# Second-layer expert weights laid out eight rows per partition, three experts moved as one transfer each

## The chip, the cores and the metric

The kernel runs on one core of a Trainium2 chip. The time is the device time of one execution in microseconds (us). In this document PE is TensorE, PEld its weight loads, DVE VectorE, ACT ScalarE, POOL GpSimd and SP SyncE, which issues every DMA (transfer) of this kernel. Less is better.

## The reference

An attention with 32 memory slots per head feeds a soft mixture of 8 experts. The change lies in the experts:

```python
    logits = x @ phi
    d = np.exp(logits - logits.max(0, keepdims=True))
    d /= d.sum(0, keepdims=True) + 1e-09
    slot_input = (d.T @ x).reshape(E, S_per_e, D)
    for e in range(E):
        h = np.maximum(slot_input[e] @ w1[e], 0.0)
        slot_out[e] = h @ w2[e]
    ...
    return (c @ slot_out).astype(np.float32)
```

Here x has 4608 rows of 512 columns, E is 8, each expert has 4 slots, w1[e] is 512 x 1024 and w2[e] is 1024 x 512, all float32. The two weight sets are 16 MB each. A slot row passes through w1, a ReLU and w2, and the output mixes the 32 slot rows for each of the 4608 rows.

## The kernel before

The kernel first runs attention and routing for four pairs of batches, then the experts, then the output. A planner (class Plan) takes all steps with estimated costs and a priority, simulates the engines, and emits each engine's instructions in the order it finds. A wait in front of an instruction holds everything behind it on its engine.

**First layer** (expert_in, L1383). Each expert's w1 comes as two transfers of 1 MB, 8 KB per partition. One transfer feeds 8 matmuls. The stationary operand is 32 columns wide, so a matmul uses one of four 32-column strips of the array, named by tile_position (0, 32 j); j picks which quarter of the 1024 hidden columns the strip makes. The moving operand of 256 columns is read from the weights in pairs of floats, one pair in every four floats.

**Second layer** (expert_out and mult, L1432). w2[e] comes in halves of 512 rows, four rows per partition, again 1 MB with 8 KB per partition. A half is multiplied twice, once for each half d of the 512 output columns: into kvbank for d = 0, into scbank for d = 1. I call one call of mult a product: four matmuls of 256 columns. In the kernel before its loop over k and j writes strip x = 2 k + j, so the four matmuls go to strips 0, 1, 2, 3. Each strip adds up its own partial sum over all experts, and slot_sums (L1347, L1355) adds the four strips up at the end.

**Tails.** The last NT = 5 of the 16 halves are loaded in pieces of 256 KB (tail_out): first ten pieces for d = 0, then ten for d = 1. The output for the first 256 columns can then start while the pieces for the others still arrive. The five d = 0 products close kvbank. Then PE does slot_sums(0), two direct outputs (L1572), and the outputs of six groups (out_mult, L1588) with the five d = 1 products placed between them by the table RIGHT. After the last of these slot_sums(1) follows, then the d = 1 outputs of the same groups, then 18 outputs of full width.

**Outputs.** ACT and DVE copy each output from its bank to a staging tile (L1564, L1565), and SP stores the tile (L1601). A group of three is stored as one transfer of 384 KB for each d. A store waits for its copies, and all stores and loads stand in one SP queue in the planner's order.

**Buffers.** The weight loads take slots of 2048 floats per partition (ws) in one arena; a slot is free again when the product that reads it has run. Loads rotate over eight semaphores, so a load also waits until the eighth load before it has landed.

Of the kernel before, what the change touches and what calls it, by code (L numbers as in the profile page):

```python
# [16 lines left out]
PE, DVE, ACT, POOL, SP = range(5)  # L17
# [253 lines left out]
def kernel(  # L271
# [27 lines left out]
    E, DM, FF = w1.shape  # L299
    NS = moe_phi.shape[1]  # L300
# [18 lines left out]
    add = plan.add  # L319
# [21 lines left out]
    W_SZ = 2048  # L341
# [12 lines left out]
    early = []  # L354
# [14 lines left out]
    def area(off, shape, n, below=(), fifo=False):  # L369

        size = shaped(off, shape)[1][1]
        xs = [shaped(off + i * size, shape) for i in range(n)]
        return Slots([a for a, _ in xs], [r for _, r in xs], below, fifo)
# [126 lines left out]
    def load(dst, src, nbytes, w, pri=None):  # L500
        add(
            SP, 0.06, lambda: nc.sync.dma_start(dst(), src), w=[w],  # L502
            dma=nbytes / {1 << 20: DMA_RATE, 1 << 18: HALF_RATE}.get(nbytes, IN_RATE), pri=pri, slack=SPREAD if nbytes == 1 << 18 else 0.0,
        )


# [781 lines left out]
    NW = (ARENA - small) // W_SZ  # L1288
    W0 = ARENA - NW * W_SZ
    ws = area(W0, [W_SZ], NW, early)  # L1290
    ots = area(W0, [OT_SZ], NOUT, [ws])
    b0 = W0 + NOUT * OT_SZ
    big = {6: area(b0, [6 * DM], 1, [ws]), 9: area(b0 + 6 * DM, [9 * DM], 1, [ws])}
    wqs = Slots(
        [qtile[:, i * W_SZ: i * W_SZ + W_SZ] for i in range(2)],
        [(TOP + i * W_SZ, W_SZ) for i in range(2)], [qs],
# [26 lines left out]

    EG = 4
    NT, NA = 5, 6
    RIGHT = (-1, 1, 1, 2, 2)
    SLOT_AT = (20.06, 20.08, 20.1)
    hTb = hTs.tile().split(E // EG)
# [3 lines left out]
    def load_w(src, pool=ws):  # L1332
        t = pool.tile()
        load(lambda: t.ap, src, 1 << 20, t)
        return t
# [38 lines left out]
    def expert_in(e, hb):  # L1374
        w1v = w1[e].rearrange("(i p z) f -> i p (z f)", i=2, z=2)
        w1b = [load_w(w1v[i], wqs if e == EG else ws) for i in range(2)]
        for i in range(2):

            def f(i=i):
                wv = w1b[i].ap.rearrange("p (c f) -> p c f", c=2)  # L1380
                for c in range(2):
                    for j in range(4):
                        nc.tensor.matmul(  # L1383
                            hb.ap[NS * j: NS * j + NS, :256],
                            SIM.ap[:, 2 * i + c, NS * e: NS * e + NS],
                            wv[:, c, 512 * (j // 2): 512 * (j // 2) + 512].rearrange(
                                "p (x u t) -> p x u t", u=2, t=2
                            )[:, :, j % 2, :],
                            start=(e % EG == 0 and i == 0 and c == 0),
                            stop=(e % EG == EG - 1 and i == 1 and c == 1),  # L1390
                            tile_position=(0, NS * j),
                        )

            add(PE, (0.9, 32), f, r=[SIM, w1b[i]], w=[hb])
# [27 lines left out]

    tails = []

    def mult(dst, e, i, t, d):
        u = 2 * e + i
        wide = t.ap.rearrange("p (j t d) -> p j t d", j=2, t=2)
        for k in range(2):
            for j in range(2):

                x = 2 * k + j
                nc.tensor.matmul(  # L1432
                    dst[NS * x: NS * x + NS, :HD],
                    hT()[:, 4 * k + 2 * i + j, NS * e: NS * e + NS],
                    wide[:, j, k, d * HD: d * HD + HD],
                    start=(u == 0),
                    stop=(u == 2 * E - 1),
                    tile_position=(0, NS * x),
                )

    def expert_out(e):
        w2v = w2[e].rearrange("(i p x) d -> p i (x d)", i=2, x=4)
        for i in range(2):
            t = ws.tile()
            if 2 * e + i >= 2 * E - NT:
                tails.append((e, i, t.split(4)))
                continue
            load(
                lambda t=t: t.ap, w2v[:, i], 1 << 20, t,
            )  # L1450
            for d in range(2):
                add(
                    PE, (0.45, 16),
                    lambda d=d, e=e, i=i, t=t: mult(pacc[d].ap[:, 0], e, i, t, d),
                    r=[hTb.part(e // EG), t], w=[pacc[d]],
                )

    def tail_out():
        for d in range(2):
            for e, i, t in tails:  # L1460
                w2h = w2[e].rearrange("(i p j t) d -> p i j t d", i=2, j=2, t=2)
                for j in range(2):
                    load(
                        lambda j=j, d=d, t=t: t.ap.rearrange("p (j t d) -> p j t d", j=2, t=2)[
                            :, j, :, d * HD: d * HD + HD
                        ],
                        w2h[:, i, j, :, d * HD: d * HD + HD], 1 << 18, t.part(2 * d + j),
                    )

    def tail_mult(d, n, after=()):  # L1470
        e, i, t = tails[n]
        return add(
            PE, (0.45, 16), lambda: mult(pacc[d].ap[:, 0], e, i, t, d),
            r=[hTb.part(e // EG), t.part(2 * d), t.part(2 * d + 1)], w=[pacc[d]], after=after,
        )


# [210 lines left out]
```

## Time and profile before

| what | value |
|---|---|
| time of the kernel, median of 3 runs | 201.5 us (201.01 to 202.52) |
| profiled execution, first to last instruction (its span) | 199.7 us |
| PE busy | 169.6 us, 85% of the span |
| DVE busy | 141.1 us, 71% |
| transfers moved | 76.47 MB, mean 383 GB/s |

The profile has no time of its own for the profiled execution beside its span; the median of the runs is 1.8 us longer than that span. The page cuts the span into 40 slices and gives for each the busy share of every engine and of the 16 DMA engines. "Chain" is the chain of waits that ended last, followed back from the last instruction. A float32 matmul stands in the trace as two records, one for each of two passes, each with a weight load of its own; the rows count records. The end of a matmul record is modelled, its start is not. In a view by windows the count of a window holds every instruction that was running in it.

### The profile page before, as it was taken

The page shows a single profiled execution, that of the slowest core. Times are in us where ns is not written, and L with a number is a line of the kernel's source. Part 1 is how long each engine was busy: PE and PEld are TensorE (multiplying, and loading weights), DVE is VectorE, ACT ScalarE, POOL GpSimd, SP SyncE. Part 2 cuts the span into 40 slices and gives each one's busy share as a digit, 9 for nine tenths or more (in the row PEclk, how much of TensorE's full clock was granted, in tenths as well). Part 3 has the DMA queues.
Part 4 walks back from the last instruction along what each step waited for, and adds up shares of the span by engine and source line. Part 5 has one row for each costly group of instructions (what it writes and reads, how often), then busy time and mean ns, then how long its engine had stood idle before and what let it go on. Part 6 is the DMA issues. An engine that isn't in the chain of part 4 may idle for free.

```text
span 199.7 us, 6103 instructions
## 1 busy us (share of the span) xinstructions
PE 169.6 (85%) x2607; PEld 109.4 (55%) x2607; DVE 141.1 (71%) x267; ACT 74.5 (37%) x191; POOL 95.6 (48%) x92
## 2 busy tenths in 40 slices
PE   7999737978879899787999799799999998999900
PEld 6777534544547487464666357565756633467500
DVE  7822631499999899899899997378999800658810
ACT  2032314436371755606553243110229500356600
POOL 7189303489995994889963276100016950000000
PEclk9999996699999999999999999999999999999965
DMA  6999999999999999999999999999999999999995
GB/s 200 366 391 395 382 384 390 381 390 381 402 364 388 391 379 403 382 390 404 420 422 410 415 420 420 417 423 427 415 418 425 365 322 328 344 317 344 398 447 255
DMA packets 32075, 76.47 MB, mean 383 GB/s; under 512 B 2097, under 2 KB 15921, under 8 KB 28337
## 3 DMA queue, kind: packets, MB, share of 16 engines
q1 hardware_dynamic: 32048, 76.09, 100.4%
q8 instruction: 20, 0.33, 0.7%
q14 instruction: 7, 0.05, 0.1%
HBM read 66.65 MB, written 9.44 MB: 381 GB/s over the span
## 4 chain that ended last, share of the span: by engine, by line
PE 34%; DMA 25%; POOL 16%; DVE 9%; issue 5%; SPq 4%; ACT 2%; POOLq 0%; DVEq 0%; ACTq 0%
DMA arena<-in_moe_w_dram 12%; DMA arena<-in_v_dram 9%; PE bank L1588 6%; POOL arena L871 5%; POOL arena L669 4%; POOL arena L848 4%; PE scbank L813 4%; DMA arena<-in_phi_dram 4%; PE bank L882 4%; PE kvbank L704 4%; SPq L502 4%; PE bank L1383 4%; POOL arena L648 3%; PE bank L1010 2%; PE scbank L1432 1%
## 5 line engine op out<-in xcount | busy, mean ns | idle before, releaser
L648 POOL TENSOR_TENSOR arena<-arena 128x1152 f32<-128x1152 f32 x8 | 21.0, 2631 | 17.1 <-ACT arena L641 14.0
L591 DVE STREAM_TRANSPOSE arena<-top 128x1152 f32<-128x1152 f32 x16 | 21.6, 1354 | 8.2 <-DMA top<-in_q_dram 8.2
L520 PE MATMUL kvbank<-ones 128*128 128x256 f32 x82 | 24.6, 439 | 2.4 <-ACT arena L728 1.3
L704 PE MATMUL kvbank<-arena 64*32 64x128 f32 x1152 | 20.7, 273 | 6.6 <-ACT arena L657 2.6
L669 POOL TENSOR_TENSOR arena<-arena 128x128 f32<-128x128 f32 (+2 forms) x32 | 23.4, 730 | 3.2 <-ACT arena L657 1.3
L813 PE MATMUL scbank<-arena 64*64 64x288 f32 x256 | 23.1, 434 | 2.1 <-DVE arena L827 2.0
L1526 POOL TENSOR_TENSOR cT<-cS,cT 32x640 fp32r<-32x640 f32 (+1 forms) x8 | 11.3, 1416 | 26.1 <-ACT cT L1521 25.7
L871 POOL TENSOR_TENSOR arena<-arena,ssm 128x576 f32<-128x576 f32 x16 | 18.3, 1151 | 9.6 <-DVE ssm L867 7.9
L848 POOL TENSOR_TENSOR arena<-arena,smx 128x576 f32<-128x576 f32 x16 | 18.4, 1151 | 8.0 <-DVE smx L843 8.0
L704 PEld LDWEIGHTS kvbank<-arena 64*32 64x32 f32 x1152 | 16.1, 105 | 10.9 <-issue 4.7
L606 DVE TENSOR_REDUCE arena<-arena 128x128 f32<-128x1152 f32 x8 | 17.1, 2146 | 4.6 <-DMA arena<-in_phi_dram 4.6
L520 PEld LDWEIGHTS kvbank<-ones 128*128 128x128 f32 x82 | 16.5, 216 | 6.4 <-ACT arena L728 1.7
L882 PE MATMUL bank<-arena 128*128 128x288 f32 x64 | 18.6, 423 | 1.0 <-DVE arena L874 0.8
L1565 DVE COPY arena<-bank 128x256 f32<-128x256 f32 (+1 forms) x30 | 14.4, 510 | 4.9 <-PE bank L1588 4.3
L827 DVE STREAM_TRANSPOSE arena<-scbank 128x576 f32<-128x576 f32 x16 | 12.2, 763 | 6.3 <-PE scbank L813 6.2
L1588 PE MATMUL bank<-sr,cT 64*128 64x256 f32 (+1 forms) x100 | 15.1, 358 | 0.4 <-ACT arena L1564 0.2
L813 PEld LDWEIGHTS scbank<-arena 64*64 64x64 f32 x256 | 9.6, 138 | 9.9 <-DVE arena L827 3.3
L853 ACT ACTIVATE arena<-arena 128x576 f32<-128x576 f32 x16 | 10.9, 684 | 10.3 <-POOL arena L848 10.3
L882 PEld LDWEIGHTS bank<-arena 128*128 128x128 f32 x64 | 11.2, 189 | 5.9 <-issue 1.7
L1588 PEld LDWEIGHTS bank<-sr,cT 64*128 64x128 f32 x100 | 9.9, 184 | 6.5 <-DVE arena L1565 4.1
L1564 ACT COPY arena<-bank 128x256 f32<-128x256 f32 (+1 forms) x24 | 10.4, 445 | 8.2 <-PE bank L1588 7.1
L1383 PE MATMUL bank<-arena,SIM 128*32 128x256 f32 x224 | 13.2, 390 | 0.2 <-DVE SIM L1264 0.2
(135 smaller groups left out, 266.4 us busy)
## 6 DMA issues: line engine op xcount, KB each, us to landing
arena<-in_moe_w_dram SPq DMA_DIRECT2D x25, 1024.0 KB, 13.7
top<-in_q_dram SPq DMA_DIRECT2D x8, 1152.0 KB, 11.4
arena<-in_k_dram SPq DMA_DIRECT2D x8, 1152.0 KB, 10.3
arena<-in_v_dram SPq DMA_DIRECT2D x8, 1152.0 KB, 12.7
arena<-in_moe_w_dram SPq DMA_DIRECT2D x20, 256.0 KB, 5.8
arena<-in_phi_dram SPq DMA_DIRECT2D x8, 576.0 KB, 6.8
out_dram<-arena SPq DMA_DIRECT2D x10, 384.0 KB, 4.4
out_dram<-arena SPq DMA_DIRECT2D x1, 2304.0 KB, 8.1
```

The costliest lines, as they stand in the source:

```text
L520: lambda: nc.tensor.matmul(warm.ap, ones, ones.unsqueeze(1).to_broadcast([P, 2, P]), start=True, stop=True,),
L591: lambda: nc.vector.transpose(qT.ap.rearrange("p (i u y) -> p u i y", i=2, y=Y), qt.ap[:, h * QT_SZ: h * QT_SZ + QT_SZ].rearrange("p (u i ...
L606: lambda: nc.vector.tensor_reduce(mx.ap[:, c0:c1], ph().rearrange("p c j m -> p c m j"), axis=AX.X, op=ALU.max),
L648: lambda: nc.gpsimd.tensor_tensor(ph(), ph(), mb.ap[:, c0:c1].unsqueeze(2).to_broadcast([P, c1 - c0, J, M]), op=ALU.subtract,),
L669: plus = lambda o, x, y: nc.gpsimd.tensor_tensor(o, x, y, op=ALU.add)
L704: nc.tensor.matmul(acc.ap[M * c: M * c + M, a, : 2 * D], ph()[h0: h0 + HALF, c, j, :], kv()[h0: h0 + HALF, :, c, j * D: j * D + D], start= ...
L813: nc.tensor.matmul(scb.ap[HALF * g: HALF * g + HALF, a, :JY], pair[g].kd.ap[h0: h0 + HALF, i, c].rearrange("p r m -> p (r m)"), pair[g].qT ...
L848: lambda: nc.gpsimd.tensor_tensor(exv(), exv(), bc(mx), op=ALU.subtract),
L871: lambda: nc.gpsimd.tensor_tensor(exv(), exv(), bc(sm), op=ALU.mult),
L882: nc.tensor.matmul(lp.ap[:, :JY], vpb.ap[:, h, :], aT.ap[:, a * JY: (a + 1) * JY], start=(h == 0), stop=(h == H - 1),)
L1383: nc.tensor.matmul(hb.ap[NS * j: NS * j + NS, :256], SIM.ap[:, 2 * i + c, NS * e: NS * e + NS], wv[:, c, 512 * (j // 2): 512 * (j // 2) + ...
L1588: nc.tensor.matmul(po.ap[:, : x.stop - x.start], cT[bp].ap[y: y + HALF, j // 2 * P: j // 2 * P + P], sr.ap[y: y + HALF, t, x], start=(t == 0),
```

## The change

w2[e] is now laid out with eight rows per partition: partition p holds rows 8 p to 8 p + 7, 16 KB without a break. Half h of an expert is then not 512 rows of the matrix but the first or the second four rows of every partition.

- Experts 0 and 1 (ONES = 2) still come as two transfers of 1 MB each, into two ws slots.
- Experts 2, 3 and 4 come as one transfer of 2 MB each, 16 KB per partition, into one slot of the new pool w2s, which lies over two neighbouring ws slots.
- Expert 5 takes a w2s slot too. Its first half comes as 1 MB; its second half and experts 6 and 7 come as the same twenty 256 KB pieces as before, now from rows that are 16 KB apart in memory instead of 8 KB.
- So that hidden unit and weight row meet, the first layer reads one pair in every eight floats (j = 4 groups of pairs), and mult takes its weights and strips in another way: product (e, h, d) writes strips x = 2 h and 2 h + 1, each for k = 0 and for k = 1.

The number of matmuls, weight loads, copies and bytes is the same. There are three transfers fewer.

```diff
@@ -1288,9 +1288,10 @@
     NW = (ARENA - small) // W_SZ
     W0 = ARENA - NW * W_SZ
     ws = area(W0, [W_SZ], NW, early)
-    ots = area(W0, [OT_SZ], NOUT, [ws])
+    w2s = area(W0, [2 * W_SZ], NW // 2, [ws, *early])
+    ots = area(W0, [OT_SZ], NOUT, [w2s])
     b0 = W0 + NOUT * OT_SZ
-    big = {6: area(b0, [6 * DM], 1, [ws]), 9: area(b0 + 6 * DM, [9 * DM], 1, [ws])}
...
+    ONES = 2
...
@@ -1383,9 +1385,7 @@
                         nc.tensor.matmul(
                             hb.ap[NS * j: NS * j + NS, :256],
                             SIM.ap[:, 2 * i + c, NS * e: NS * e + NS],
-                            wv[:, c, 512 * (j // 2): 512 * (j // 2) + 512].rearrange(
-                                "p (x u t) -> p x u t", u=2, t=2
-                            )[:, :, j % 2, :],
+                            wv[:, c].rearrange("p (x j t) -> p x j t", j=4, t=2)[:, :, j, :],
                             start=(e % EG == 0 and i == 0 and c == 0),
                             stop=(e % EG == EG - 1 and i == 1 and c == 1),
                             tile_position=(0, NS * j),
...
@@ -1422,56 +1422,70 @@
 
     tails = []
 
-    def mult(dst, e, i, t, d):
-        u = 2 * e + i
-        wide = t.ap.rearrange("p (j t d) -> p j t d", j=2, t=2)
+    def mult(dst, e, h, t, d):
+        n = 2 if e < ONES else 4
+        wide = t.ap.rearrange("p (j t d) -> p j t d", j=n, t=2)
         for k in range(2):
-            for j in range(2):
-
-                x = 2 * k + j
+            for x in range(2 * h, 2 * h + 2):
                 nc.tensor.matmul(
                     dst[NS * x: NS * x + NS, :HD],
-                    hT()[:, 4 * k + 2 * i + j, NS * e: NS * e + NS],
-                    wide[:, j, k, d * HD: d * HD + HD],
-                    start=(u == 0),
-                    stop=(u == 2 * E - 1),
+                    hT()[:, 4 * k + x, NS * e: NS * e + NS],
+                    wide[:, x % n, k, d * HD: d * HD + HD],
+                    start=(e == 0 and k == 0),
+                    stop=(e == E - 1 and k == 1),
                     tile_position=(0, NS * x),
                 )
 
     def expert_out(e):
-        w2v = w2[e].rearrange("(i p x) d -> p i (x d)", i=2, x=4)
-        for i in range(2):
-            t = ws.tile()
-            if 2 * e + i >= 2 * E - NT:
-                tails.append((e, i, t.split(4)))
+        w2v = w2[e].rearrange("(p x) d -> p (x d)", x=8)
+        if e < ONES:
+            for h in range(2):
+                t = load_w(w2v[:, h * W_SZ: h * W_SZ + W_SZ])
+                for d in range(2):
+                    add(
+                        PE, (0.45, 16),
+                        lambda d=d, h=h, t=t: mult(pacc[d].ap[:, 0], e, h, t, d),
+                        r=[hTb.part(e // EG), t], w=[pacc[d]],
+                    )
+            return
+        t = w2s.tile().split(8)
+        whole = [h for h in range(2) if 2 * e + h < 2 * E - NT]
+        if len(whole) == 2:
+            load(lambda: t.ap, w2v, 1 << 21, t)
+        elif whole:
+            load(
+                lambda: t.ap[:, :W_SZ], w2v[:, :W_SZ], 1 << 20,
+                [x for i in range(4) for x in t.part(i)],
+            )
+        for h in range(2):
+            if h not in whole:
+                tails.append((e, h, t))
                 continue
-            load(
-                lambda t=t: t.ap, w2v[:, i], 1 << 20, t,
-            )
             for d in range(2):
                 add(
                     PE, (0.45, 16),
-                    lambda d=d, e=e, i=i, t=t: mult(pacc[d].ap[:, 0], e, i, t, d),
-                    r=[hTb.part(e // EG), t], w=[pacc[d]],
+                    lambda d=d, h=h: mult(pacc[d].ap[:, 0], e, h, t, d),
+                    r=[hTb.part(e // EG), *(t.part(4 * h + i) for i in range(4))], w=[pacc[d]],
                 )
...
 
     def tail_out():
         for d in range(2):
-            for e, i, t in tails:
-                w2h = w2[e].rearrange("(i p j t) d -> p i j t d", i=2, j=2, t=2)
-                for j in range(2):
+            for e, h, t in tails:
+                w2h = w2[e].rearrange("(p j t) d -> p j t d", j=4, t=2)
+                for x in range(2 * h, 2 * h + 2):
                     load(
-                        lambda j=j, d=d, t=t: t.ap.rearrange("p (j t d) -> p j t d", j=2, t=2)[
-                            :, j, :, d * HD: d * HD + HD
+                        lambda x=x, d=d, t=t: t.ap.rearrange("p (j t d) -> p j t d", j=4, t=2)[
+                            :, x, :, d * HD: d * HD + HD
                         ],
-                        w2h[:, i, j, :, d * HD: d * HD + HD], 1 << 18, t.part(2 * d + j),
+                        w2h[:, x, :, d * HD: d * HD + HD], 1 << 18, t.part(4 * h + 2 * d + x % 2),
...
 
     def tail_mult(d, n, after=()):
-        e, i, t = tails[n]
+        e, h, t = tails[n]
         return add(
-            PE, (0.45, 16), lambda: mult(pacc[d].ap[:, 0], e, i, t, d),
-            r=[hTb.part(e // EG), t.part(2 * d), t.part(2 * d + 1)], w=[pacc[d]], after=after,
+            PE, (0.45, 16), lambda: mult(pacc[d].ap[:, 0], e, h, t, d),
+            r=[hTb.part(e // EG), *(t.part(4 * h + 2 * d + i) for i in range(2))],
+            w=[pacc[d]], after=after,
```

The load order at the place where the second layer begins shows the larger transfers. These are SP's rows of the kernel before, from the first half of expert 2 (first row) on to the first piece of the tail:

```order
L502 DMA arena<-in_moe_w_dram 128x2048 [waits DMAHW5_49,PE_49,Pool_49]
L502 DMA arena<-in_moe_w_dram 128x2048 [waits DMAHW6_49]
L502 DMA arena<-in_moe_w_dram 128x2048 [waits DMAHW7_49,PE_49]
L502 DMA arena<-in_moe_w_dram 128x2048 [waits DMAHW0_49,PE_49]
L502 DMA arena<-in_moe_w_dram 128x2048 [waits DMAHW1_49,PE_49]
L502 DMA arena<-in_moe_w_dram 128x2048 [waits DMAHW2_49,PE_49]
L502 DMA arena<-in_moe_w_dram 128x2048 [waits DMAHW3_49,PE_49]
L502 DMA arena<-in_moe_w_dram 128x2x256 [waits DMAHW4_49,PE_49]
```

And these are SP's rows of the changed kernel at the same place:

```order
L502 DMA arena<-in_moe_w_dram 128x4096 [waits DMAHW5_49,PE_49,Pool_49]
L502 DMA arena<-in_moe_w_dram 128x4096 [waits DMAHW6_49,PE_49]
L502 DMA arena<-in_moe_w_dram 128x4096 [waits DMAHW7_49,PE_49]
L502 DMA arena<-in_moe_w_dram 128x2048 [waits DMAHW0_49,PE_49]
L502 DMA arena<-in_moe_w_dram 128x2x256 [waits DMAHW1_49,PE_49]
```

Six transfers of 2048 floats per partition have become three of 4096; the rest keeps its order. The second of them now waits for PE, where the row before it had no such wait.

PE's order of steps does not change. These are PE's rows of the kernel before where the last d = 0 product ends and the first d = 1 product stands between outputs (kvbank and scbank hold the sums of the second layer, bank_62 and so on the outputs):

```order
L1432 MATMUL kvbank<-arena 32x256 [waits DMAHW4_49]
L1432 MATMUL kvbank<-arena 32x256 [waits DMAHW5_49]
L1432 MATMUL kvbank<-arena 32x256 x2
L1355 MATMUL bank_65<-cS,rep 128x256 [waits DVE_49]
L1572 MATMUL bank_63<-cS 128x256
L1572 MATMUL bank_64<-cS 128x256
L1432 MATMUL scbank<-arena 32x256 [waits DMAHW6_49]
L1432 MATMUL scbank<-arena 32x256 [waits DMAHW7_49]
L1432 MATMUL scbank<-arena 32x256 x2
L1588 MATMUL bank_62<-sr,cT 128x256 [waits Activation_49,Pool_49]
L1588 MATMUL bank_62<-sr,cT 128x256 [waits DVE_49]
```

And these are the rows of the changed kernel there:

```order
L1430 MATMUL kvbank<-arena 32x256 [waits DMAHW1_49]
L1430 MATMUL kvbank<-arena 32x256 [waits DMAHW2_49]
L1430 MATMUL kvbank<-arena 32x256 x2
L1357 MATMUL bank_65<-cS,rep 128x256 [waits DVE_49]
L1586 MATMUL bank_63<-cS 128x256
L1586 MATMUL bank_64<-cS 128x256
L1430 MATMUL scbank<-arena 32x256 [waits DMAHW3_49]
L1430 MATMUL scbank<-arena 32x256 [waits DMAHW4_49]
L1430 MATMUL scbank<-arena 32x256 x2
L1602 MATMUL bank_62<-sr,cT 128x256 [waits Activation_49,Pool_49]
L1602 MATMUL bank_62<-sr,cT 128x256 [waits DVE_49]
```

Nothing has moved but line numbers and the names of the semaphores. What differs does not stand in these rows: before, the four matmuls of a product go to strips 0, 1, 2, 3; now they go to strips 2, 3, 2, 3 (or 0, 1, 0, 1 where h is 0).

## Rows read from the trace of the kernel before

**Rows 1.** The page: the span, and the DMA engines' busy tenths in 40 slices.

```profile
span 199.7 us, 6103 instructions
...
DMA  6999999999999999999999999999999999999995
```

**Rows 2.** Chain in order of time, from 160 us: start us, us, what.

```profile
161.67 5.71 DMA arena<-in_moe_w_dram
...
167.43 0.67 PE kvbank L1432 x6
...
170.16 0.57 PE scbank L1432 x8
...
175.61 0.61 PE scbank L1432 x8
...
176.25 0.38 ACT cS L1347
...
189.78 0.69 DVE arena L1565
```

**Rows 3.** Windows: stretch, its us, busy us (count) of each engine, PEclk, DMA share, GB/s.

```profile
136.60:151.60 15.00, 14.99 (x258) 9.51 (x262) 13.85 (x37) 4.65 (x12) 2.25 (x2) 1.00 1.02 419
...
161.80:167.40 5.60, 4.93 (x38) 1.12 (x30) 0.00 (x0) 0.00 (x0) 1.04 (x1) 1.00 1.01 330
...
188.90:192.40 3.50, 0.84 (x3) 0.29 (x2) 1.35 (x3) 0.59 (x1) 0.00 (x0) 0.88 1.01 427
...
174.35:174.85 0.50, 0.50 (x9) 0.10 (x8) 0.42 (x1) 0.00 (x0) 0.00 (x0) 1.00 0.41 141
177.15:177.65 0.50, 0.50 (x5) 0.42 (x4) 0.00 (x0) 0.24 (x1) 0.00 (x0) 1.00 0.38 127
177.80:197.50 19.70, 11.73 (x71) 7.48 (x69) 10.76 (x21) 7.68 (x16) 0.00 (x0) 0.85 1.04 399
```

**Rows 4.** Timeline of PE: start us, us, engine, line, operation, tiles, shapes, count.

```profile
155.74 0.61 PE L1432 MATMUL kvbank<-arena 128*32 128x256 f32 x8
156.17 0.61 PE L1432 MATMUL scbank<-arena 128*32 128x256 f32 x8
```

**Rows 5.** Windows with kvbank's instructions alone, where a product begins at 156.60.

```profile
156.60:156.63 0.03, 0.03 (x4) 0.02 (x4) 0.00 (x0) 0.00 (x0) 1.00 1.88 751
156.60:156.81 0.21, 0.21 (x4) 0.13 (x4) 0.00 (x0) 0.00 (x0) 1.00 0.73 276
```

**Rows 6.** Windows with line L781 alone: matmuls on one and the same tile.

```profile
109.36:109.39 0.03, 0.03 (x2) 0.03 (x3) 1.00 0.00 0
...
109.36:109.50 0.14, 0.14 (x4) 0.14 (x5) 1.00 1.39 585
```

**Rows 7.** Windows with line L1588 alone: outputs that alternate between two row tiles.

```profile
170.66:170.68 0.03, 0.02 (x2) 0.02 (x2) 1.00 0.94 328
...
170.66:170.98 0.33, 0.32 (x4) 0.32 (x6) 1.00 1.08 350
```

**Rows 8.** Windows with line L704 alone: eight matmuls on eight tiles, in the program's order.

```profile
58.60:58.66 0.06, 0.05 (x8) 0.06 (x12) 1.00 1.20 446
```

**Rows 9.** Timeline of weight loads at the last d = 0 piece, with the wait before them.

```profile
166.69 0.14 PEld L1432 LDWEIGHTS kvbank<-arena 128*32 128x32 f32 x2 [0.57 <-DMA arena<-in_moe_w_dram]
167.43 0.15 PEld L1432 LDWEIGHTS kvbank<-arena 128*32 128x32 f32 x6 [0.61 <-DMA arena<-in_moe_w_dram]
```

**Rows 10.** Matmuls of two lines: duration ns min/median/max, first and last start us.

```profile
L1383 PE MATMUL bank<-arena,SIM x224: 385/388/413, 136.6 to 151.6; 128*32 128x256 f32 x112
...
L1432 PE MATMUL kvbank<-arena x128: 377/379/403, 151.7 to 167.7; 128*32 128x256 f32 x128
```

**Rows 11.** SP's waits from 130 to 168 us, and loads issued from 140 us on.

```profile
SPq L502 <- PE bank L1383: 7.4, 7, 4.7
...
arena<-in_moe_w_dram SPq DMA_DIRECT2D x2, 1024.0 KB, 17.9
```

**Rows 12.** Timeline of ACT: the copy of the last d = 0 group.

```profile
176.65 0.37 ACT L1564 COPY arena<-bank 128x256 f32<-128x256 f32 x1
```

More of the change, by code (lines that the diff above doesn't have):

```diff
@@ L502, in load @@
             SP, 0.06, lambda: nc.sync.dma_start(dst(), src), w=[w],
-            dma=nbytes / {1 << 20: DMA_RATE, 1 << 18: HALF_RATE}.get(nbytes, IN_RATE), pri=pri, slack=SPREAD if nbytes == 1 << 18 else 0.0,
+            dma=nbytes / {1 << 21: DMA_RATE, 1 << 20: DMA_RATE, 1 << 18: HALF_RATE}.get(nbytes, IN_RATE), pri=pri, slack=SPREAD if nbytes == 1 << 18 else 0.0,
         )
@@ L1290 @@
     ws = area(W0, [W_SZ], NW, early)
-    ots = area(W0, [OT_SZ], NOUT, [ws])
+    w2s = area(W0, [2 * W_SZ], NW // 2, [ws, *early])
+    ots = area(W0, [OT_SZ], NOUT, [w2s])
     b0 = W0 + NOUT * OT_SZ
-    big = {6: area(b0, [6 * DM], 1, [ws]), 9: area(b0 + 6 * DM, [9 * DM], 1, [ws])}
+    big = {6: area(b0, [6 * DM], 1, [w2s]), 9: area(b0 + 6 * DM, [9 * DM], 1, [w2s])}
     wqs = Slots(
```

## Prediction

> **What bounds the kernel now.** The page comes first: the DMA engines are busy in every slice but the last few tenths [rows 1], so a shorter transfer looks like the way to a shorter kernel. But that row is an average over 16 engines and 5 us. Windows inside the output stage show two stretches of half a microsecond in which the DMA share falls to 0.41 and 0.38, from 174.35 and from 177.15 us [rows 3]. There the loads are over and the next store is not yet ready. After 177.8 us the share is 1.04 without a break until the end [rows 3]. So the end is a fixed stretch of stores of about 20 us, and it begins when PE and the copies release the d = 0 store that starts at 177.7. That store waits for the copy which ends at 177.02 [rows 12], and the copy for an output that PE makes behind the last d = 1 product.
>
> The chain of waits tells who is late there. From 161.67 to 167.39 it is the last d = 0 load. From 167.43 on it is PE almost without a gap: the last d = 0 product (0.67 us), then slot_sums and outputs with five d = 1 products between them, the first at 170.16 and the last at 175.61, 0.57 to 0.61 us each, then a copy at 176.25 [rows 2]. The chain never goes back to a load there. So in this stage whatever a product takes longer moves the end.
>
> **What a product costs, before and now.** A product begins every 0.43 us and has eight records [rows 4]: four matmuls of two passes. Four records start within 0.03 us, and no fifth has started 0.21 us after the first [rows 5]. So a round of four lasts 0.216 us, and a product is two rounds. Four can run at once only because they go to four strips. On one and the same tile records start one after the other: at L781, with 64 columns, two more start in the 0.11 us after the window that holds two [rows 6], so 0.055 us each, a quarter of 0.216 for a quarter of the columns. In the changed mult the four matmuls of a product go to two strips, two on each. Each strip then runs four passes in a row: four rounds, 0.86 us. A product that stands alone costs 0.43 us more.
>
> Whether that is paid depends on what PE can start meanwhile. L1588 gives two matmuls to one row tile and the next two to the other; yet two records start within 0.02 us and the third and fourth follow within 0.32 us [rows 7]. (out_mult: y is 0 or 64 by the parity of j). So PE starts the first matmul of the free tile before the second of the busy one. The weight loads of a tail product stand as x2 for the matmul whose piece landed first and x6 for the other three [rows 9], so the two passes of a matmul stand next to each other in the queue. At L704 eight first passes start within 0.06 us [rows 8]: the eighth stands 14 records behind the first, with seven second passes between that have not started.
>
> - **Products of the 11 whole halves** (151.7 to 161.8 us). Products of h = 0 use strips 0 and 1, those of h = 1 strips 2 and 3. Eight matmuls for the first pair are followed by eight for the second: 16 records lie between the first of each. With a reach of about 15 records the two pairs run beside each other nearly all the time. Laid out round by round with that reach, two products take 0.88 to 0.92 us instead of 0.865; I take +0.2 us over 11 halves, and at most +0.6. This is hidden: PE waits for d = 0 pieces from 161.8 to 167.4. Four of the five last d = 0 products need 4 x 0.86 = 3.4 us of these 5.6, so some 2.1 us are free.
> - **The last d = 0 product** begins when its second piece lands at 167.39. Three matmuls are left to it, two of them on one strip: four rounds instead of two, **+0.43 us** on the chain.
> - **The five d = 1 products** stand alone between outputs that use the array in row tiles (64*128). Each takes four rounds: **5 x 0.43 = +2.15 us** on the chain. Copies don't hide it: each waits for PE.
>
> **What the larger transfers give.** Loads in 8 KB pieces move 419 GB/s, stores of 12 KB per partition 427 [rows 3]. Three loads of 2 MB, 6.3 MB, at 427 instead of 419 take 0.28 us less; three completions are gone too. If pieces of 16 KB run no faster it is nothing. I take **-0.2 us**, between 0 and -0.3. It moves the landing at 167.39.
>
> **What else moves.** The 2 MB loads wait for two products of the first layer instead of one, of which PE finishes 16 in 15.0 us [rows 3], one every 0.94 us. SP waited up to 4.7 us for such a release and the loads behind it still took 17.9 us to land [rows 11]; one needs 2.5 us alone (1 MB at 419 GB/s). So the queue holds over ten microseconds of work, and a release 0.94 us later leaves no gap. A whole expert is ready at once instead of half by half. PE is behind the loads there (14.99 of 15.00 us busy [rows 3]) and loses nothing; if it had to wait 2.5 us, 0.4 us would stick out behind the 2.1. Pieces from rows 16 KB apart have no row here; bounds are nothing and, if they lost a tenth of the 5.7 us that the last ones take [rows 2], +0.6 us. I take nothing, since rates follow the piece size in all rows. The three DMA issues fewer on SP cost and give nothing, as SP waits there anyway.
>
> The first layer reads a pair in every eight floats instead of every four. Its matmuls take 388 ns now, those that read without a step 379 [rows 10]: 2% for the first step. Nothing here has the new step. From 0 to 10% of 15.0 us, 1.5 us, stays inside the 2.1 us free; I take nothing on the path. The Trainium skill ("SBUF — State Buffer", Door 1) says that reads within a 16-byte line are free and each new line costs something. Before and now each pair lies in a line of its own, so by that rule nothing changes, and no run here shows a wider step yet.
>
> **Sum.** -0.2 + 0.43 + 2.15 = +2.4 us at the copy of 177.02. The stores behind it are one unbroken stretch, so the end moves as much, less a little: in the two dips six of 16 engines still worked off older pieces (0.38 to 0.41) and have some slack. I take +2.3. Span 199.7 becomes 202.0. The median of the runs lies 1.8 us above that span, so 201.5 becomes **203.8 us**, +1.1%. About 1% is what a measurement can tell from no change, so the mark for slower is 203.5.
>
> **Rivals.**
> - *The four rounds don't show: not slower.* If two matmuls on one strip cost no more than on two (the bound being 54 ns a record, whichever strip), a product stays at 0.43 us and only -0.2 is left: **201.3 us**. For it: the trace doesn't name strips. Against it: [rows 6] has one record after the other on one tile. It decides from 2.0 us: a product between outputs must stay under some 0.95 us from its start to the next output for the kernel to stay within 1%.
> - *PE doesn't reach ahead far enough.* If it starts nothing past the product in hand, each of 22 whole products costs 0.43 us more, +9.5 us, of which 2.1 are free: +7.4 at the d = 0 sum and +2.4 as above: **about 211 us**. Half of that loss gives 206.5. For it: [rows 7] proves a reach of two records only. Against it: [rows 8]. It bites once the products cost 0.1 us more each. The Trainium skill ("TensorE: Matmul & The Clock Gate", Part 3, The mechanism) says that matmuls start and end strictly in order and only weight loads are pulled ahead; by that rule this rival would hold, with its 211 us. [rows 7] disagrees: a matmul starts ahead of an earlier one.
> - *Loads decide after all.* Pieces of 16 KB or rows 16 KB apart run otherwise than I think and outweigh the rest: 201 or 205 us.
>
> **How the numbers follow.** The forecast, both terms of the tail paid in full or nearly so: 0.70, own range 202.6 to 204.8, of which 0.20 below 203.5. No doubling: 0.13. Short reach: 0.12. Loads decide: 0.05, 0.03 of it faster. That gives faster 0.03, same 0.33 (0.20 + 0.13), slower 0.64 (0.50 + 0.12 + 0.02). The range takes the forecast and the case of no doubling: 201.2 to 205.0.
>
> **What would show it.** In the changed profile each scbank product between outputs takes about 1.0 us instead of 0.57, the last kvbank product 1.1 instead of 0.67. Two products of the whole halves still take 0.87 to 0.95 us; 1.7 would mean the second rival. The last d = 0 piece lands 0 to 0.3 us earlier. The two dips of the DMA share behind the loads grow by about 2.5 us together, and the stretch of stores behind them stays at about 20 us. The forecast is wrong if products between outputs stay near 0.6 us, if the first layer takes over 17 us, or if the last d = 0 piece lands later than before.

## The result and the profile after

The changed kernel takes 203.5 us (median of 6 runs, 203.28 to 204.38); the kernel before, run beside it, 202.0 us (6 runs, 200.90 to 204.29). The ratio is 1.0104, 95% interval 1.0074 to 1.0135. So it is slower, by 1.5 to 2.7 us; the interval does not exclude that it is by less than 1%. (The ratio itself means 2.1 us. The two medians differ by 1.5, but the runs of the kernel before scatter by 3.4.) The ratios of this document leave out two executions that took longer than the rest of their kernel, one of 306.62 us with four strips and one of 205.13 us with all loads of 2 MB. The profiled execution took 203.85 us with a span of 202.1, 2.4 more than [rows 1]. Its page, span and DMA slices:

```profile
span 202.1 us, 6096 instructions
...
DMA  6999999999999999999999999999999999689996
```

The last row has two new low digits, 6 and 8, in the slices from 172 to 182 us, where [rows 1] has nines. The chain of waits from 161 us on (start, us, what) stands against [rows 2]:

```profile
161.55 6.13 DMA arena<-in_moe_w_dram
167.68 0.04 issue
167.72 1.06 PE kvbank L1430 x6
...
170.85 0.99 PE scbank L1430 x8
171.84 0.68 PE bank L1602 x8
172.52 0.99 PE scbank L1430 x8
...
177.97 0.99 PE scbank L1430 x8
...
192.55 0.69 DVE arena L1579
```

The line numbers are shifted: mult is L1430 (before L1432), the outputs L1602 (before L1588), their copies L1578 and L1579. The product behind the last d = 0 piece takes 1.06 us instead of 0.67; the five scbank products between outputs take 0.99 instead of 0.57, the last of them instead of 0.61. The output groups beside them are as before, 0.68 us for eight records. The last entry, a copy, is at 192.55 instead of 189.78: 2.77 us later.

Windows of the output stage (stretch, its us, busy us of PE, PEld, DVE, ACT and POOL with counts, PEclk, DMA share, GB/s) answer [rows 3]:

```profile
175.60:176.80 1.20, 0.99 (x8) 0.67 (x10) 1.00 (x3) 0.44 (x2) 0.00 (x0) 1.00 0.05 17
...
180.40:182.00 1.60, 1.60 (x12) 0.97 (x10) 1.19 (x4) 0.88 (x3) 0.00 (x0) 1.00 0.79 269
182.00:183.40 1.40, 1.40 (x12) 1.11 (x12) 1.23 (x4) 0.74 (x2) 0.00 (x0) 1.00 0.70 233
183.40:200.10 16.70, 8.86 (x50) 5.53 (x48) 8.34 (x16) 6.19 (x12) 0.00 (x0) 0.87 1.03 403
```

For 1.2 us from 175.6 the DMA engines do next to nothing (share 0.05). There are further gaps (0.79, 0.70) until 183.4; only then is the share full.

### The profile page after: what moved, and what is told of

Its sections match the earlier page's. It is cut to its first block, busy times and chain, and to the rows that moved or that the text cites. A ratio compares the mean times of both kernels' runs of the same rounds, so it can differ in the third digit from the quotient of the medians.

```text
span 202.1 us, 6096 instructions
## 1 busy us (share of the span) xinstructions
PE 171.5 (85%) x2607; PEld 110.2 (55%) x2607; DVE 141.0 (70%) x267; ACT 74.7 (37%) x191; POOL 95.6 (47%) x92
## 2 busy tenths in 40 slices
DMA packets 31642, 76.47 MB, mean 378 GB/s; under 512 B 2048, under 2 KB 15872, under 8 KB 28288
## 4 chain that ended last, share of the span: by engine, by line
PE 38%; DMA 20%; POOL 16%; DVE 10%; issue 6%; SPq 4%; ACT 2%; POOLq 0%; DVEq 0%
DMA arena<-in_moe_w_dram 12%; DMA arena<-in_v_dram 8%; PE bank L1602 7%; PE scbank L813 5%; PE kvbank L704 4%; POOL arena L669 4%; POOL arena L871 4%; SPq L502 4%; PE bank L882 4%; POOL arena L848 4%; PE bank L1385 3%; POOL arena L648 3%; PE scbank L1430 2%; PE bank L1010 2%; DVE arena L827 1%
## 5 line engine op out<-in xcount | busy, mean ns | idle before, releaser
L704 PE MATMUL kvbank<-arena 64*32 64x128 f32 x1152 | 20.6, 273 | 6.4 <-issue 2.6
L520 PE MATMUL kvbank<-ones 128*128 128x256 f32 x82 | 23.2, 419 | 2.4 <-ACT arena L728 1.3
L704 PEld LDWEIGHTS kvbank<-arena 64*32 64x32 f32 x1152 | 16.1, 105 | 10.7 <-issue 5.5
L1579 DVE COPY arena<-bank 128x256 f32<-128x256 f32 (+1 forms) x30 | 14.4, 510 | 7.0 <-PE bank L1602 6.4
L520 PEld LDWEIGHTS kvbank<-ones 128*128 128x128 f32 x82 | 15.6, 205 | 5.9 <-ACT arena L728 1.7
L1602 PE MATMUL bank<-sr,cT 64*128 64x256 f32 (+1 forms) x100 | 15.1, 358 | 0.5 <-ACT arena L1578 0.2
L1430 PE MATMUL scbank<-arena 128*32 128x256 f32 x128 | 15.5, 381 | 0.0
L1430 PE MATMUL kvbank<-arena 128*32 128x256 f32 x128 | 15.1, 384 | 0.4 <-DMA arena<-in_moe_w_dram 0.2
L1578 ACT COPY arena<-bank 128x256 f32<-128x256 f32 (+1 forms) x24 | 10.4, 445 | 9.9 <-PE bank L1602 9.0
```

Source lines behind the costliest of these rows:

```text
L520: lambda: nc.tensor.matmul(warm.ap, ones, ones.unsqueeze(1).to_broadcast([P, 2, P]), start=True, stop=True,),
L704: nc.tensor.matmul(acc.ap[M * c: M * c + M, a, : 2 * D], ph()[h0: h0 + HALF, c, j, :], kv()[h0: h0 + HALF, :, c, j * D: j * D + D], start= ...
L1430: nc.tensor.matmul(dst[NS * x: NS * x + NS, :HD], hT()[:, 4 * k + x, NS * e: NS * e + NS], wide[:, x % n, k, d * HD: d * HD + HD], start=( ...
L1602: nc.tensor.matmul(po.ap[:, : x.stop - x.start], cT[bp].ap[y: y + HALF, j // 2 * P: j // 2 * P + P], sr.ap[y: y + HALF, t, x], start=(t == 0),
```

## The experiments

All ratios are to the kernel before, run on the same chip in the same series.

### Four strips in the changed kernel

```diff
             for x in range(2 * h, 2 * h + 2):
+                z = 2 * k + x % 2
                 nc.tensor.matmul(
-                    dst[NS * x: NS * x + NS, :HD],
+                    dst[NS * z: NS * z + NS, :HD],
...
-                    start=(e == 0 and k == 0),
-                    stop=(e == E - 1 and k == 1),
-                    tile_position=(0, NS * x),
+                    start=(e == 0 and h == 0),
+                    stop=(e == E - 1 and h == 1),
+                    tile_position=(0, NS * z),
```

The four strips hold partial sums that slot_sums adds up, so any strip may take any term.

> The changed kernel, but the four matmuls of a product go to four strips again (strip 2k + x%2 instead of x); its rows, loads and columns stay those of the change. Theory (two strips per product cost 0.43 us each time a product stands alone): products between outputs return from 0.99 to about 0.57 us, the last d = 0 product from 1.06 to 0.67, and 6 x 0.42 = 2.5 us go: 203.5 becomes 201.0 to 201.3, ratio to the kernel before 0.995 to 1.000. Rival (the layout costs the time: pieces from rows 16 KB apart, wider column step, 2 MB loads): stays at 203.5, ratio 1.010, or in between by what the layout costs.

Measured: 200.89 us, ratio 0.9974 (0.9955 to 0.9994). Its chain of waits:

```profile
167.15 0.04 issue
167.19 0.67 PE kvbank L1431 x6
...
169.93 0.57 PE scbank L1431 x8
...
175.37 0.61 PE scbank L1431 x8
...
189.55 0.69 DVE arena L1580
```

The products are back at 0.67 and 0.57 us, and the last copy is 3.0 us earlier than in the changed kernel; 0.5 of that is an earlier landing of the last d = 0 piece (167.15 against 167.68), with the very same loads. The whole loss goes with the strips alone. What is left of the change is a small gain over the kernel before; this version beats both.

### Two strips in the kernel before

```diff
-                x = 2 * k + j
+                x = 2 * i + j
...
-                    start=(u == 0),
-                    stop=(u == 2 * E - 1),
+                    start=(e == 0 and k == 0),
+                    stop=(e == E - 1 and k == 1),
```

> The kernel before, but the four matmuls of a product go to two strips (2i + j for both k); layout, loads and columns stay those of before. Theory: 5 x 0.43 between outputs and 0.43 at the last d = 0 product, +2.4 to +2.6 us, 202.0 becomes 204.4, ratio 1.012, a little above the changed kernel because its larger transfers are not there. Rival (layout or loads make the difference): 202.0, ratio 1.000.

Measured: 203.97 us, ratio 1.0135 (1.0093 to 1.0176). The same loss comes with the old layout and the old loads; in the chain:

```profile
167.27 1.06 PE kvbank L1432 x6
...
170.40 0.99 PE scbank L1432 x8
```

With the first experiment this closes the case both ways: strips without layout cost 2.7 us (1.9 to 3.5), layout without strips costs nothing.

### Four strips for the whole halves alone

```diff
+                z = 2 * k + x % 2 if 2 * e + h < 2 * E - NT else x
```

(with dst and tile_position by z; start at e = 0, h = 0; stop as in the changed kernel.)

> The changed kernel, with four strips for the products of the 11 whole halves alone; the pieces' products (5 of d = 0, 5 of d = 1) keep two. Theory (whole halves run side by side on the two pairs of strips and end before the d = 0 pieces land): no change against the changed kernel, 203.5, ratio 1.010, although the products of whole halves go back to 0.43 us in a row. Rival (the whole halves are not hidden, PE comes late to the d = 0 pieces): 202 to 203, ratio 1.002 to 1.006.

Measured: 203.25 us, ratio 1.0091 (1.006 to 1.0121). The changed kernel's is 1.0104, and each lies inside the other's interval. So the two strips cost nothing measurable in the whole halves. They are paid at the pieces.

### All whole halves on one pair of strips

```diff
+                z = x % 2 if 2 * e + h < 2 * E - NT else x
```

(with dst and tile_position by z, and a start at the first pieces' products for strips 2 and 3.)

> The changed kernel, with all 22 products of the whole halves on strips 0 and 1; none of the other half's matmuls can then run beside them. The pieces' products are those of the change. Theory (PE starts matmuls of a free pair ahead of those queued for a busy one, and this alone hides the whole halves): 22 x 0.99 = 21.8 us from 152.1, so to 174 us instead of about 162; the five d = 0 pieces' products follow, 2 to 4 us; the last ends at 176 to 178 instead of 168.8, and the kernel at 210 to 213 us, ratio 1.04 to 1.055. Rival (PE works in order and the doubled products were paid in the changed kernel already): as the changed kernel, 203.5, ratio 1.010.

Measured: 209.77 us, ratio 1.0399 (1.0361 to 1.0437), a little under the expected range. PE's timeline (start, us, engine, line, operation, tiles, shapes, count) and the chain behind it:

```profile
170.15 1.03 PE L1431 MATMUL scbank<-arena 128*32 128x256 f32 x8
171.02 1.03 PE L1431 MATMUL kvbank<-arena 128*32 128x256 f32 x8
...
172.56 2.11 PE L1431 MATMUL kvbank<-arena 128*32 128x256 f32 x34
```

```profile
173.99 0.74 PE kvbank L1431 x14
174.73 0.02 issue
```

With no other pair to work on, a product begins every 0.86 us; I had expected 0.99, which is the chain's figure for one that stands alone with its start and end. The last d = 0 product ends at 174.73 instead of 168.78, 5.95 us later, and the span is 5.9 us longer (208.0 against 202.1). What the whole halves lose is free up to a point, and these rows tell where it lies. The last 34 records of the d = 0 sum (two of the first piece product and all of the other four) begin at 172.56; in the timeline of the changed kernel they begin at 163.97 and still wait for pieces:

```profile
163.97 2.82 PE L1430 MATMUL kvbank<-arena 128*32 128x256 f32 x26
167.03 1.75 PE L1430 MATMUL kvbank<-arena 128*32 128x256 f32 x8 [0.24 <-DMA arena<-in_moe_w_dram]
```

They begin 8.59 us later and end 5.95 later, so 2.64 us were free behind the whole halves of the changed kernel, and the rest passes to the end. With all pieces there, the 34 records need 2.17 us (172.56 to 174.73): the piece products, too, run side by side on the two pairs.

### One more test of how far PE reaches ahead

The whole halves of experts 0 to 3 in another order: the products of all h = 0 first, those of h = 1 behind. The lines that set the order:

```diff
+        for h, d, a, k in sorted(held, key=lambda x: x[0]):
+            add(*a, **k)
```

> The changed kernel (two strips), with the order of whole halves changed: first h = 0 of experts 0 to 3 (8 products, 64 records, on strips 0 and 1), then h = 1 of them (8 products on strips 2 and 3), then the rest as before. Theory (PE starts a matmul of a free pair up to about 15 records ahead): only the last 2 products of the first block run beside the first 2 of the second; the first six take 0.86 us each and the 16 products 12 us, to about 164 instead of 159. Rival 1 (it reaches much further, 64 records or more): the two blocks run side by side, 16 products in 7 to 7.5 us. Rival 2 (it reaches one product only): no more than one product overlaps, 13 us.

Measured: one run, 204.87 us. PE's timeline at the seam of the two blocks:

```profile
156.47 1.03 PE L1430 MATMUL scbank<-arena 128*32 128x256 f32 x8
157.33 1.03 PE L1430 MATMUL kvbank<-arena 128*32 128x256 f32 x8
158.20 0.39 PE L1430 MATMUL scbank<-arena 128*32 128x256 f32 x2
158.21 0.41 PE L1430 MATMUL kvbank<-arena 128*32 128x256 f32 x2
...
159.10 1.03 PE L1430 MATMUL scbank<-arena 128*32 128x256 f32 x8
159.96 1.03 PE L1430 MATMUL kvbank<-arena 128*32 128x256 f32 x8
```

The first product for strips 2 and 3 (kvbank at 158.21) starts with the very last product of the first block, not with the one before it at 157.33. The rest of the second block then runs alone again. From 151.66 the 16 products take 13.5 us (the last begins at 164.28 and has four rounds), of which 0.4 are transposes: rival 2 holds and my theory, a reach of 15 records, is wrong. Yet in [rows 8] a matmul started 14 records ahead. The difference: there seven of those records had not started; here, one round earlier, all eight of the last product had not.

### What the reach counts

```diff
+                u, m = 2 * e + h, 2 * k + x % 2
+                z = ((0, 1, 2, 0), (1, 3, 2, 3))[d][m] if u < 2 * E - NT else x
```

(with dst and tile_position by z, and a start at the first product of each strip.)

> The changed kernel; in the whole halves a kvbank product now uses strips 0, 1, 2, 0 and the scbank product behind it 1, 3, 2, 3. The first record for strip 3 is the eleventh, with seven before it that have not started when the first three run (the second passes of three matmuls, two passes for strip 0 and two for strip 1). Theory A (what counts is how many records in front have not started, and eight can wait, which fits both the eight tiles of the attention part and the order experiment): where PE begins afresh, at the first product, one scbank record starts together with three kvbank records, within some 0.03 us. Theory B (what counts is how far behind the oldest record that has not started it stands, up to eight): the first scbank record starts one round later, 0.21 us. Theory C (about 15 records in order, the figure of the prediction): as A here, but C has been contradicted by the order experiment. Kernel time as the changed kernel or a little under, 203 to 204 us.

Measured: one run, 203.18 us. PE's timeline where the first product begins:

```profile
153.09 0.39 PE L1433 MATMUL kvbank<-arena 128*32 128x256 f32 x3
153.12 0.40 PE L1433 MATMUL scbank<-arena 128*32 128x256 f32 x1
153.31 0.39 PE L1433 MATMUL kvbank<-arena 128*32 128x256 f32 x3
153.35 0.38 PE L1433 MATMUL scbank<-arena 128*32 128x256 f32 x1
```

One scbank record starts 0.03 us behind the first kvbank records, not a round later. It stands nine behind the oldest record that has not started, so theory B falls. Theory A fits this, the seam and [rows 8]: a record starts when its strip is free and fewer than eight records in front of it have not started. That the number is eight rests on these three places. A product has eight records too, so a rule that counts products (PE reaches into the next one and no further) would give the same rows here and at the seam; no run tells the two apart.

The order experiment also confirms the free time found with one pair. The same 34 records begin there at 167.66, 3.69 us later than in the changed kernel, and end at 169.83, 1.05 later. Again 2.64 us were free:

```profile
167.66 2.11 PE L1430 MATMUL kvbank<-arena 128*32 128x256 f32 x34
```

### What the layout gains: packets of 8 and 16 KB

The version with four strips, and the five whole experts' loads all of 1 MB (ONES = 5):

> The changed kernel with four strips (first experiment), and experts 2 to 4 as two loads of 1 MB each instead of one of 2 MB; rows per partition and columns stay those of the change. Theory (the larger packets give the gain: in the profile a 16 KB packet takes 613 ns and two of 8 KB 624, 24 per engine, so 0.26 us): 0.26 us longer than the first experiment, ratio to the kernel before 0.998 to 1.000. Rival (the gain of the first experiment has nothing to do with the size of the transfers): ratio stays at 0.997.

Measured: 201.23 us, ratio 1.0004 (0.9981 to 1.0028). By the ratio the gain is not to be seen without the 2 MB loads, as the theory has it. But the interval overlaps the first experiment's, and the chain doesn't bear the theory out: the last d = 0 piece landed no later than in the first experiment (167.15), where the theory had 0.26 us.

```profile
167.09 0.04 issue
167.13 0.67 PE kvbank L1431 x6
```

So neither the size of the gain, some 0.3%, nor its cause is settled by this.

All five as 2 MB (ONES = 0):

> The changed kernel with four strips, and all five whole experts in one load of 2 MB each. Theory (each 2 MB load saves 8 x 11 ns = 0.09 us): 0.18 us less than the first experiment, ratio 0.996 to 0.997. Rival (the first loads of 2 MB need two free buffers side by side, are issued later and leave a gap): the last d = 0 piece lands later than 167.2 and the ratio is 1.000 or more.

Measured: 203.32 us, ratio 1.0077 (1.0045 to 1.0108): the rival holds. SP's waits (engine, line, what for, us in total, times, longest) from 118 to 135 us, and windows over the place:

```profile
SPq L502 <- DVE arena L874: 9.2, 1, 9.2
```

```profile
128.00:131.00 3.00, 2.61 (x19) 1.51 (x25) 1.82 (x6) 0.72 (x3) 0.00 (x0) 1.00 0.94 328
...
134.00:137.00 3.00, 2.81 (x50) 1.87 (x49) 2.38 (x10) 0.00 (x0) 0.00 (x0) 1.00 1.00 360
```

The same rows with four strips and ONES = 2:

```profile
SPq L502 <- DVE arena L874: 3.6, 1, 3.6
```

```profile
128.00:131.00 3.00, 2.61 (x26) 1.61 (x33) 1.65 (x6) 0.90 (x3) 0.00 (x0) 1.00 0.99 410
...
134.00:137.00 3.00, 2.79 (x52) 1.85 (x55) 2.43 (x9) 0.00 (x0) 0.00 (x0) 1.00 1.01 421
```

SP waits 9.2 us, ahead of a 2 MB load, for DVE to release a buffer of the attention part; with ONES = 2 it waits 3.6 for the same line, ahead of a load of 1 MB. The first load of the stretch so leaves at 128.00 instead of 122.06. The DMA engines move 328 GB/s instead of 410 in the first window and 360 instead of 421 in the second. Together that is 0.43 MB less, or 1.0 us at 410 GB/s, by my estimate. In the chain the product behind the last d = 0 piece starts at 168.19, 1.0 us later than with ONES = 2. That is half of the 2.1 us between the two ratios. The profiled execution (201.97 us) is one of the two shortest of its kernel's eight, which run from 201.91 to 205.13; these rows don't show the other half, nor why the runs scatter so.

### The step of the first layer's reading

The version with four strips, whose first layer takes a pair in every sixteen floats. It so takes other columns than it should, as many as before.

```diff
-                            wv[:, c].rearrange("p (x j t) -> p x j t", j=4, t=2)[:, :, j, :],
+                            w1b[i].ap.rearrange("p (x j t) -> p x j t", j=8, t=2)[:, :, 4 * c + j, :],
```

> The changed kernel with four strips, and the first layer's matmuls read a pair in every sixteen floats instead of every eight; it takes the wrong columns of the first layer, as many as before, so its times hold and its numbers do not matter. The change from four to eight cost 2 to 4 ns of 390 per matmul by the profiles. Theory (the step of the reading costs next to nothing): at most 4 ns more per matmul, the first layer at 15.2 to 15.4 us, ratio as in the first experiment, 0.997. Rival (it rises with the step and was only just hidden): 10 ns or more each, first layer 15.7 us or more; still hidden up to some 2 us, so to be read from the rows rather than from the ratio.

Measured: 200.89 us, ratio 0.9975 (0.9964 to 0.9987). The matmuls of the first layer (duration min/median/max, first and last start), first with a pair in every eight floats (changed kernel), then in every sixteen:

```profile
L1385 PE MATMUL bank<-arena,SIM x224: 390/391/418, 136.9 to 151.9; 128*32 128x256 f32 x112
```

```profile
L1385 PE MATMUL bank<-arena,SIM x224: 376/377/406, 136.8 to 151.2; 128*32 128x256 f32 x112
```

From four to eight floats a matmul goes from 388 [rows 10] to 391 ns; with sixteen it is 377. The cost does not rise with the step, and the ratio stays that of the first experiment. The rule of the Trainium skill ("SBUF — State Buffer", Door 1), by which nothing changes as long as each pair lies in a line of its own, agrees with the first two figures to 3 ns; the drop to 377 it doesn't give.

## Why the prediction was right, step by step

- **A product alone costs 0.43 us more: right.** In the chain it is 0.42 for four of the five d = 1 products (0.57 to 0.99), 0.38 for the last of them (0.61 to 0.99) and 0.39 for the last d = 0 product (0.67 to 1.06). The terms 2.15 and 0.43 measured 2.06 and 0.39. The first two experiments show that the strips are the cause, in both directions.
- **The whole halves hide theirs: right in effect, wrong in size and reason.** I took +0.2 us, at most +0.6. PE's timeline of the changed kernel:

```profile
152.10 1.04 PE L1430 MATMUL kvbank<-arena 128*32 128x256 f32 x8
152.96 0.39 PE L1430 MATMUL scbank<-arena 128*32 128x256 f32 x2
152.98 0.41 PE L1430 MATMUL kvbank<-arena 128*32 128x256 f32 x2
...
153.87 1.03 PE L1430 MATMUL scbank<-arena 128*32 128x256 f32 x8
...
155.20 1.06 PE L1430 MATMUL kvbank<-arena 128*32 128x256 f32 x8
...
163.28 0.39 PE L1430 MATMUL scbank<-arena 128*32 128x256 f32 x2
```

  And of the kernel before, the first product of the whole halves and the first behind them:

```profile
151.74 0.65 PE L1432 MATMUL kvbank<-arena 128*32 128x256 f32 x8
...
161.78 2.54 PE L1432 MATMUL kvbank<-arena 128*32 128x256 f32 x18
```

  Three products run alone: the first, the one ahead of the transposes and the one behind them. Eight records wait in front of any that could use the other pair. From then on two run side by side, 0.90 us for both, but not h = 0 beside h = 1 of one d as I had laid them out: a product runs beside the next one in the program when that is on the other pair. From 152.10 to about 164.15 (163.28 and four rounds) they take 12.05 us instead of 10.04 (151.74 to 161.78 before), **+2.0 us**. The step that failed is "with a reach of about 15 records": [rows 8] was read as a distance, where records that had not started count. It did no harm, but the 2.1 us that the prediction held free is not the reason: that would have left 0.1 us, and 2.64 were still free behind the 2.0 (the experiments with one pair and with the other order; some 0.3 of it by the late landing in this profile). The prediction took four d = 0 products one after another, 4 x 0.86 = 3.4 us. Where their pieces are there, they run side by side as well, and with two records more take 2.17. So two sizes were wrong here, in opposite directions, and that the term came out at nothing on the path is in part luck.
- **The larger transfers: not to be seen in one execution, −0.5 us by the ratios.** I took -0.2, from 0 to -0.3. In the profile of the changed kernel the last d = 0 piece lands at 167.68, 0.29 later than in [rows 2], which the prediction named as a sign against it. With the very same loads it landed at 167.15 with four strips, at 167.12 with the step of sixteen and at 167.03 in the test of what the reach counts, 0.24 to 0.36 earlier than in [rows 2]. So with one and the same set of loads it scatters by some 0.6 us between executions, more than the term. With loads of 1 MB alone it stood at 167.39 [rows 2], 167.23 (two strips in the kernel before, whose last product starts at 167.27) and 167.09, which is no later on the whole. By the ratios of the version with four strips and of the one with the step of sixteen, the layout with four strips gains 0.26% or 0.25%, 0.5 us (0.1 to 0.9, and 0.3 to 0.7). The ratios have the sign of the term, at about twice its size. That the packets make this gain is not shown: the ratio of the run with 1 MB loads speaks for it, its interval leaves it open, and the landings don't show it.
- **The sum.** In this profile 0.29 + 0.39 + 2.06 = 2.74 us; the last copies are 2.77 later. With 2.45 us for the products and the 0.5 that the layout gains by the ratios it is 2.0 us, and the changed kernel's ratio gives 2.1.
- **The end moves as much: right, but not as described.** I had a stretch of stores without a break behind the second dip. It is not unbroken now: from 180.4 to 183.4 the DMA share is 0.79 and 0.70, where before it was 1.04 [rows 3]. Stores at that place too wait for outputs, so the products' delay is felt until 183.4. The chain runs over PE's outputs up to the last copies at 192.55, 2.77 us later than before. The span grows by 2.4, so behind the copies 0.4 us are made up, where the prediction took off 0.1.
- **Rivals.** That the four rounds don't show is refuted by 0.99 us in the chain. That PE doesn't reach ahead is refuted by the pairs: kvbank at 152.98 starts while six records of the scbank product of 152.96 still wait. The Trainium skill's rule ("TensorE: Matmul & The Clock Gate", Part 3, The mechanism) that matmuls start strictly in order does not hold in these rows; the 211 us of this rival were not tested as such, but the experiment with one pair, where hardly anything can run side by side, took 209.8 us. The Trainium skill's statement that tiles work independently ("TensorEngine Tiling (Array Packing)", Key Properties) agrees with them, up to the eight that wait. That loads decide is refuted by the second experiment, which loses as much with the old loads.
- **Row pitch, longer waits of the 2 MB loads, and the step of the first layer at nothing: right** for the change as it is. The version with four strips, which has all three, is no slower than the kernel before. That waits of the 2 MB loads are harmless depends on ONES = 2: with 2 MB from expert 0 on they cost 2 us.

## What to carry to other kernels

When a layout change alters which strip of the array a matmul uses, count the strips of each group of matmuls that stands alone on the chain. Here two strips instead of four took a group from 0.57 to 0.99 us. Inside a long run the same doubling is mostly hidden if the next matmuls in the program are on the other strips: two groups took 0.90 us together instead of 0.86. Where the strips only hold partial sums, choose them apart from the layout; here that turned a loss of 1% into a small gain. A larger transfer may pay a little in packets, which these runs don't settle, and can cost more in the wait for its larger buffer.

## What the runs showed of the hardware

- PE starts matmuls for free strips ahead of earlier ones for busy strips, and what limits it is the number of earlier records that have not started: fewer than eight, at the three places shown, not the distance in the program. A limit of one product ahead, which has eight records here, is not ruled out.
- What 16 KB packets save against 8 KB ones is too little to be settled here: with four strips, three 2 MB loads against six of 1 MB gave 0.9974 and 1.0004, with intervals that overlap, and the last piece landed at 167.15 and 167.09 us.
- A float32 matmul whose moving operand takes a pair in every sixteen floats took 377 ns, less than with every eight (391) or every four (388 [rows 10]). I have no cause for it.
